# Attention and SwiGLU block, forward and backward, on one core: one burst of loads a group in the backward queue, x and partial sums in the rows of the job operands, row layouts of q and k stored in the forward

## The chip, the core and the metric

The kernel runs on one core of one Trainium2 chip. The core has five engines that run side by side, each with its own queue of instructions: TensorE (PE, matmuls and transposes into PSUM), VectorE (DVE), ScalarE (ACT), GpSimd (POOL) and SyncE (SP). SP does no arithmetic here: it issues most of the DMA transfers, in the order in which they stand in its queue, and POOL issues most of the others. The metric is the time of one execution on the device in microseconds (us), lower is better; the median of several executions counts.

## The reference

The forward is a layer norm followed by two branches that are added to the input, multi-head attention (16 heads of 28, 2048 positions) and a SwiGLU feed-forward (width 448 to 1792). The kernel returns the output and the gradients for x and the five weights.

```python
def _A_ref(x, wqkv, wo):
    ...
    scores = jnp.einsum("bhqd,bhkd->bhqk", q, k) * (Dh ** -0.5)
    p = _softmax(scores, axis=-1)
    o = jnp.einsum("bhqk,bhkd->bhqd", p, v)
    ...
def _B_ref(x, w_gate, w_up, w_down):
    g = _silu(x @ w_gate)
    u = x @ w_up
    return (g * u) @ w_down
x = A_x
xn = _layernorm(x, axis=-1)
return x + _A_ref(xn, A_wqkv, A_wo) + _B_ref(xn, B_w_gate, B_w_up, B_w_down)
...
_out, _vjp = jax.vjp(_f, A_x, A_wqkv, A_wo, B_w_gate, B_w_up, B_w_down)
_grads = _vjp(grad_out)
```

## The kernel before

The kernel has a forward loop, a backward loop and a short final stage. The order of the work is written out by hand; each engine runs its instructions in that order.

**Forward** (from the start to about 690 us). The 16 heads stand in 4 groups `g` of 4 heads, padded to 32 rows each, so that q, k and v of a group are 128 x 2048 tiles (`qT`, `kT`, `vT`, feature by position). The loop runs over `g`, 4 blocks of queries `qc` and 16 blocks of keys `kt`; each step computes scores (L667), their exponential on ACT (L671) and the product with v (L642). Beside it, `fill` takes small pieces of other work from a queue: the projections of the next group, and the feed-forward with its gradients. The feed-forward is cut into 14 slices `fc` of 128 columns and 4 blocks `sc` of positions. At the end of each item (`fc`, `sc`) SP gets one DMA transpose of the tile `hduT` (L474) and three stores of its parts to DRAM tensors, `hO_d`, `da_d` and `du_d` (L477). `hduT` has two buffers.

Twelve weight layouts (`weight_layout`) are made on the way: SP transposes a block of a weight into the tile `w_stage`, which has one buffer (L356, L358), and POOL stores it in DRAM one item later (L357, L359). One is made in each of the slices 1 to 12, at `sc == 1`, first gate, then up, then qkv. `proj_store` stores `qT`, `kT` and `vT` of a group in DRAM.

**Backward** (about 690 to 1510 us). The 512 units run over 8 pairs of heads `pr`, 4 blocks of keys `kc`, and 16 blocks of queries. Eight units make a group `W` (64 of them); `pos` is the place of a unit in its group. For each unit PE computes two score tiles (L962, L972), ACT the exponential `E` (L981), and DVE the product `ds` (L987, one instruction a unit). Two units share a buffer `ds`, and there are 5 such buffers. `ds` is needed in transposed form, `dsT`. Of the four buffers of a group three are transposed by SP (L1014, 512 KB each, at `pos` 2, 4 and 6), the fourth by PE (L901) with two copies on DVE at `pos` 1 of the next group (L903). A buffer `ds` is free again when its transpose has landed and PE has read it.

Each group also carries a **job**, a chain of matmuls that fills PE's gaps: 16 output tiles (`y`), 16 tiles each of two partial sums of the gradient of x (`dx` 0 and 1), and weight gradients (`dwq`). A job needs one block of operands, `ck`, loaded two groups ahead by `job_load` at `pos` 0 (L749 from `hO_d`, L755 from `da_d` or `du_d`). A `y` job adds x, and a `dx` 1 job adds the partial sum of `dx` 0, with one more matmul each; these 112 KB come in a load of their own into `x_c` (L751 from x, L759 from `pA_d`), 32 loads in all. `extra_load` brings, at `pos` 4, one more block in most groups: an operand of the next pair (L613, 256 KB), a row layout of q, k or dO for the next group of heads (`load_rows`, L621 and L623, 512 KB), or a piece of a weight (L603). For q and k, `load_rows` is a DMA transpose from `qT_d` or `kT_d`; for dO it is a plain load, since the forward has stored rows of dO in `spo_d`. `sp_later` holds the transposes of finished sums (L888, L939).

Loads and transposes of the backward all stand in SP's queue. The order in a group is: `ck`, `x_c` at `pos` 0; first transpose of `ds` at `pos` 2; extra load, second transpose at `pos` 4; third transpose at `pos` 6.

At the change from forward to backward the pools of the forward are closed, and the tiles of the backward are placed on the same memory; the first instruction that writes such a tile waits for the last one that used the memory.

Of the kernel before, what the change touches and what calls it, by code (L numbers as in the profile page):

```python
# [13 lines left out]
BF16 = mybir.dt.bfloat16  # L14
# [5 lines left out]
D = 448  # L20
# [3 lines left out]
G = 4  # L24
HP = 32
P = 128
NT = S // P
NFC = F // P
# [10 lines left out]
def kernel(  # L39
# [31 lines left out]
    spo_d = dram.tile([G, P, NT * P], BF16, name="spo_d")  # L71
    hO_d = dram.tile([NT, P, NFC + G, P], BF16, name="hO_d")
    da_d = dram.tile([NT, P, NFC, P], BF16, name="da_d")
    du_d = dram.tile([NT, P, NFC, P], BF16, name="du_d")
    wT_d = dram.tile([2, P, NFC, D], BF16, name="wT_d")
    wqT_d = dram.tile([P, 3 * G, D], BF16, name="wqT_d")
    pA_d = dram.tile([P, NT, D], BF16, name="pA_d")
    pB_d = dram.tile([P, NT, D], BF16, name="pB_d")
# [271 lines left out]
    def weight_layout(i):  # L350
# [8 lines left out]
        return lambda: pool.dma_start(out=wqT_d[:, :, d0:d0 + dn], in_=s_[:, :3 * G, :dn])  # L359

    queue = deque()
    cur = deque()
# [68 lines left out]
    def ffn_items(fc, sc, extra):  # L431
# [35 lines left out]
        def dh(c):  # L467
            mm("dh", lambda c: wdT[fc % 2][:, c, :], dyT, c)
            if c == 3:
                o = st["o"]  # L470
                for wi, src in ((2, "g1"), (1, "w")):
                    dve.scalar_tensor_tensor(out=o[:, :, wi, :], in0=quad(st["dh"]), scalar=0.5, in1=quad(st[src]),
                                             op0=ALU.mult, op1=ALU.mult)
                sp.dma_start_transpose(out=ffn[fc][:, tsl].rearrange("p t w s -> p (t w) s"),  # L474
                                       in_=o[:].rearrange("p t w s -> p (t w s)"))
                for wi, dst in ((0, hO_d), (1, da_d), (2, du_d)):
                    sp.dma_start(out=dst[tsl, :, fc, :].rearrange("k p s -> p k s"), in_=o[:, :, wi, :])  # L477
                if sc == 1 and 1 <= fc <= 12:
                    later.append(weight_layout(fc - 1))
                elif later:  # L480
                    later.pop()()
# [44 lines left out]
    def o_items(g, qc, o_ps):  # L526
# [8 lines left out]
        def tr(i):  # L535
# [3 lines left out]
            if i < 3:  # L539
# [12 lines left out]
                                   in_=O_sp[g][:, tsl, :].rearrange("p t c -> p (t c)"))  # L552
            sp.dma_start(out=hO_d[tsl, :, NFC + g, :].rearrange("k p s -> p k s"),
                         in_=oT[:].rearrange("p (k s) -> p k s", k=4))
# [61 lines left out]
    def load_rows(g, i):  # L616

        t = opn.tile([P, NT, P], BF16, name="Qsp", tag="v_sp") if i == 0 else \
            spg_[0].tile([P, NT, P], BF16, name=("Qsp", "Ksp", "dOsp")[i])
        if i == 2:  # L620
            sp.dma_start(out=t[:].rearrange("p t c -> p (t c)"), in_=spo_d[g])  # L621
        else:
            sp.dma_start_transpose(out=t[:], in_=(qT_d, kT_d)[i][g])  # L623
        spt[g, i] = t
# [23 lines left out]
    for i, (g, qc, kt) in enumerate(steps):  # L648
        if i == NEARLY:
            pro.close()  # L650
            open_ffn()
            proj_store(0)
        if kt == 0 and qc == (1 if g == 0 else 0) and g + 1 < G:
            push(proj_items(g + 1), front=True)
# [33 lines left out]
    while late:  # L688
        push(late.pop(0), front=True)
    fill(1e9)  # L690
    fst.close()
    bst.close()
# [50 lines left out]
    def job_load(i):  # L743
        j = jobs.get(i)
        if j is None:
            return
        if j[0] == "y":
            t = ckp.tile([P, NFC + G, P], BF16, name="ck")
            sp.dma_start(out=t[:], in_=hO_d[j[1]])  # L749
            x = ckp.tile([P, D], BF16, name="x_c")  # L750
            sp.dma_start(out=x[:], in_=x_d[:, j[1], :])  # L751
            chunk[i] = (t, x)
        elif j[0] == "dx":
            t = ckp.tile([P, NFC + G, P], BF16, name="ck")
            sp.dma_start(out=t[:, :NFC], in_=(da_d, du_d)[j[1]][j[2]])  # L755
            x = None
            if j[1] == 1:
                x = ckp.tile([P, D], BF16, name="x_c")
                sp.dma_start(out=x[:], in_=pA_d[:, j[2], :])  # L759
            chunk[i] = (t, x)  # L760

# [57 lines left out]
    def job_mms(i, ps):  # L819
# [5 lines left out]
        if j[0] == "y":  # L825
            t, x = chunk[i]
            out = []
            for n in range(NFC + G):
                rhs = (wtile["wd"][:, n, :] if n < NFC else wo_pad[:, n - NFC, :D])
                out.append(lambda n=n, rhs=rhs: pe.matmul(ps[:, :D], lhsT=t[:, n, :], rhs=rhs,  # L830
                                                          start=(n == 0), stop=False))
            out.append(lambda: pe.matmul(ps[:, :D], lhsT=ident_bf[:], rhs=x[:], start=False, stop=True))
            return out
# [4 lines left out]
        if x is not None:  # L838
            out.append(lambda: pe.matmul(ps[:, :D], lhsT=ident_bf[:], rhs=x[:], start=False, stop=True))
        return out  # L840

    def job_out(i, ps):
# [14 lines left out]
        else:  # L857
            pool.dma_start(out=(pA_d, pB_d)[j[1]][:, j[2], :], in_=o[:])

# [89 lines left out]
    for k in range(N + UW + 4):  # L949
        W, pos = k // UW, k % UW  # L950
        k_now[0] = k
        if k < N:
            pr, kc, w, qi = units[k]
            if pos == 0 and W:
                job_load(W + 2)
            if pos == 4:
                extra_load(W)
# [178 lines left out]
```

## Time and profile before

| | us |
|---|---|
| median of 3 runs | 1562.62 (1561.1 to 1566.55) |
| the profiled execution | 1575.18 |
| its span, first to last instruction | 1573.4 |
| PE busy in the span | 1438.7 (91%) |
| DVE busy | 1121.7 (71%) |
| ACT busy | 1148.8 (73%) |
| POOL busy | 293.6 (19%) |
| transposes of `ds`, issue to landing, median of 192 | 5.9 |

The times that the text takes from the profile belong to the profiled execution, which took 12.6 us longer than the median. The mean granted TensorE clock over the span is 0.958 of full speed. A row of the timeline gives start, duration, engine and line; on SP's queue a duration is the time until the next entry of the queue can be taken, not the time until the data have landed.

### The profile page before, as it was taken

The numbers are of one execution on the slowest core, as the hardware profiler recorded it, in microseconds if no ns is written. First come the engines' busy times: TensorE is split into PE (matmuls) and PEld (weight loads), VectorE is DVE, ScalarE is ACT, GpSimd is POOL, SyncE is SP. The second block draws the span as 40 slices with busy tenths as digits, with TensorE's granted clock in tenths as the row PEclk, the third lists the DMA queues.
The fourth block names the chain that finished last, engine by engine and source line by source line (L and its number), as shares of the span: only waits on it lengthen the run. The fifth ranks groups of instructions, "written<-read, shape, count | busy, mean of one in ns | idle before, by whom it ended". The sixth has DMA issues, their size and how long they took to land.

```text
span 1573.4 us, 31511 instructions
## 1 busy us (share of the span) xinstructions
PE 1438.7 (91%) x12278; PEld 580.1 (37%) x12278; DVE 1121.7 (71%) x1459; ACT 1148.8 (73%) x1312; POOL 293.6 (19%) x479
## 2 busy tenths in 40 slices
PE   6899999999999999979988899889888889999958
PEld 3233333333333333333333335333334333533424
DVE  7465556665666566648777789788888878998925
ACT  4487888887888877757667677668777777777824
POOL 4000111111111110120121122212213122221222
PEclk7688999999999999989999999999999999999979
DMA  5456638765777677859999999999999999999974
GB/s 157 110 123 140 141 76 186 148 148 118 160 147 145 142 156 158 184 138 210 216 219 211 210 195 189 221 212 208 211 214 199 203 213 196 194 213 199 195 205 134
DMA packets 764567, 276.98 MB, mean 176 GB/s; under 512 B 730929, under 2 KB 744049, under 8 KB 764417
## 3 DMA queue, kind: packets, MB, share of 16 engines
q1 hardware_dynamic: 748656, 238.19, 79.1%
q0 software_dynamic: 14960, 36.60, 8.8%
q8 instruction: 96, 1.57, 0.4%
q14 instruction: 55, 0.44, 0.1%
q10 hardware_dynamic: 800, 0.17, 0.1%
HBM read 63.44 MB, written 59.24 MB: 78 GB/s over the span
## 4 chain that ended last, share of the span: by engine, by line
PE 64%; DMA 17%; DVE 8%; ACT 6%; issue 4%; SPq 1%; POOL 0%; DVEq 0%; ACTq 0%; POOLq 0%
DMA dsT<-ds 13%; PE s_ps L667 9%; PE f_ps L412 8%; PE f_ps L438 8%; PE sd L962 6%; PE o_ps L642 5%; ACT E L981 5%; PE acc L875 5%; DVE ds L987 4%; PE aux L916 3%; PE sd L901 3%; PE f_ps L197 3%; PE sd L972 3%; PE sd L1052 2%; PE aux L830 2%
## 5 line engine op out<-in xcount | busy, mean ns | idle before, releaser
L987 DVE TENSOR_TENSOR ds<-sd,E 128x1024 bf16<-128x1024 f32 x512 | 606.4, 1219 | 126.1 <-DMA dsT<-ds 65.9
L981 ACT ACTIVATE E<-sd 128x1024 bf16<-128x1024 f32 x512 | 521.0, 1024 | 199.0 <-PE sd L972 140.8
L671 ACT ACTIVATE eT<-s_ps 128x1024 bf16<-128x1024 f32 x512 | 497.1, 1021 | 143.8 <-PE s_ps L667 142.5
L962 PE MATMUL sd<-KV,QD 32*128 32x512 bf16 x1024 | 202.7, 390 | 45.0 <-DVE ds L987 39.2
L972 PE MATMUL sd<-KV,QD 32*128 32x512 bf16 x1024 | 203.5, 390 | 11.3 <-ACT E L981 5.1
L667 PE MATMUL s_ps<-qT,kT 32*128 32x512 bf16 x1024 | 198.6, 397 | 0.4 <-ACT eT L671 0.4
L875 PE MATMUL acc<-E,dOsp 128*32 128x512 bf16 x1024 | 139.1, 395 | 3.7 <-DMA dOsp<-spo_d 3.7
L875 PE MATMUL acc<-ds,Qsp 128*32 128x512 bf16 x1024 | 139.1, 395 | 0.0
L962 PEld LDWEIGHTS <-QD 32*128 32x128 bf16 x1024 | 58.3, 91 | 206.6 <-issue 193.3
L438 PE MATMUL f_ps<-xnT,wgu 128*128 128x512 bf16 x448 | 122.3, 392 | 8.7 <-DVE w_sb L464 8.7
L836 PE MATMUL aux<-W,ck 128*128 128x448 bf16 x448 | 112.5, 356 | 0.0
L642 PE MATMUL o_ps<-eT,v_sp 128*32 128x512 bf16 x1024 | 104.4, 402 | 4.1 <-DMA v_sp<-vT 4.1
L667 PEld LDWEIGHTS <-kT 32*128 32x128 bf16 x1024 | 47.2, 91 | 164.1 <-issue 160.2
L412 PE MATMUL f_ps<-xn_sp,f_sp 128*128 128x448 bf16 x448 | 98.9, 354 | 0.0
L972 PEld LDWEIGHTS <-QD 32*128 32x128 bf16 x1024 | 69.0, 91 | 60.3 <-issue 56.3
L901 PE MATMUL sd<-ident_bf,ds 128*128 128x128 bf16 x1024 | 70.1, 223 | 20.4 <-DVE ds L987 20.0
L903 DVE COPY dsT<-sd 128x1024 bf16<-128x1024 bf16 x128 | 82.2, 684 | 2.7 <-PE sd L901 2.3
L412 PEld LDWEIGHTS <-f_sp 128*128 128x128 bf16 x672 | 58.9, 98 | 67.0 <-issue 20.2
L916 PE MATMUL aux<-dsT,Ksp 128*32 128x512 bf16 x1024 | 71.2, 398 | 7.3 <-DMA dsT<-ds 7.3
L901 PEld LDWEIGHTS <-ds 128*128 128x128 bf16 x1024 | 62.7, 100 | 35.3 <-issue 35.0
L450 DVE SCALAR_TENSOR_TENSOR g<-t_sb,f_ps 128x512 f32<-128x512 f32 x56 | 38.4, 685 | 46.1 <-ACT t_sb L448 46.1
L932 POOL TENSOR_TENSOR dq_acc<-dq_acc,dq_s 128x512 f32<-128x512 f32 x32 | 40.5, 1265 | 133.9 <-ACT dq_s L928 133.9
(145 smaller groups left out, 1719.8 us busy)
## 6 DMA issues: line engine op xcount, KB each, us to landing
ck<-hO_d SPq DMA_DIRECT2D x16, 576.0 KB, 4.7
hO_d<-hduT SPq DMA_DIRECT2D x56, 128.0 KB, 3.4
da_d<-hduT SPq DMA_DIRECT2D x56, 128.0 KB, 3.0
du_d<-hduT SPq DMA_DIRECT2D x56, 128.0 KB, 3.3
ck<-da_d SPq DMA_DIRECT2D x16, 448.0 KB, 4.5
ck<-du_d SPq DMA_DIRECT2D x16, 448.0 KB, 4.3
dq_c<-dqkv_d SPq DMA_DIRECT2D x8, 768.0 KB, 5.3
dqkv_d<-dkv_o POOLq DMA_DIRECT2D x64, 64.0 KB, 4.2
```

Source lines behind the costliest of these rows:

```text
L412: pe.matmul(acc[:, :D], lhsT=src[:, t, wi, :], rhs=rhs[:, t, :D], start=(t == 0), stop=(t == NT - 1))
L438: pe.matmul(st[name][:], lhsT=w(c), rhs=src[:, tsl, c, :], start=(c == 0), stop=(c == 3))
L642: pe.matmul(o_ps[HP * hh:HP * (hh + 1), :], lhsT=v[:, kt, HP * hh:HP * (hh + 1)], rhs=e[hh // 2][:, hh % 2, :], start=(kt == 0), stop=(kt ...
L667: pe.matmul(s_ps[:, j, :], lhsT=kT[r:r + HP, kt * P:(kt + 1) * P], rhs=qT[r:r + HP, qc * 512:(qc + 1) * 512], start=True, stop=True, tile_ ...
L671: act.activation(out=e[:], in_=s_ps[:], func=ACT.Exp, scale=SCALE)
L875: pe.matmul(acc[r:r + HP, :], lhsT=src[:, qt, 64 * hp + HP * j:64 * hp + HP * j + HP], rhs=m[:, j, :], start=(qt == 0), stop=(qt == NT - 1 ...
L901: pe.transpose(ps[:, u, i, :], ds[:, u, i // 4, (i % 4) * P:(i % 4 + 1) * P], ident_bf[:])
L916: pe.matmul(ps[r:r + HP, :], lhsT=Ks[:, kc * 4 + kt, 64 * hp + HP * j:64 * hp + HP * j + HP], rhs=dsT[:, 4 * s_:4 * s_ + 4, j, kt, :], sta ...
L962: pe.matmul(s_ps[:, j, :], lhsT=q[HP * j:HP * j + HP, qt * P:(qt + 1) * P], rhs=kv[HP * j:HP * j + HP, kc * 512:(kc + 1) * 512], start=Tru ...
L972: pe.matmul(d_ps[:, j, :], lhsT=q[r:r + HP, qt * P:(qt + 1) * P], rhs=kv[r:r + HP, kc * 512:(kc + 1) * 512], start=True, stop=True, tile_p ...
L981: act.activation(out=E[k][:], in_=s_ps[:], func=ACT.Exp, scale=SCALE)
L987: dve.tensor_tensor(out=ds[:, u % 2], in0=d_ps[:], in1=E[u][:], op=ALU.mult)
```

## The change

- The row of `hO_d` gets x behind the operands, and the row of `du_d` the partial sum of `dx` 0. x is copied from DRAM to DRAM once, by POOL, early in the forward. The 32 loads of `x_c` go, and `pA_d` with them; the loads of `ck` get longer rows (5504 and 4480 bytes a partition).
- `extra_load` moves from `pos` 4 to `pos` 0, right behind the load of `ck`.
- The row layouts of q and k are made in the forward: 16 transposes of half a tile into `w_stage` (256 KB each), each stored by POOL in `rows_d`; `load_rows` becomes a plain load for all three. A layout is made at `sc` 1 and at `sc` 3 of every slice, 28 in all: 16 row layouts at set places, and the 12 weight layouts around them, now qkv first, then gate and up. The last eight, gate and up, fall into the slices 10 to 13, and the store of the last one comes after all other work of the forward.

```diff
-    hO_d = dram.tile([NT, P, NFC + G, P], BF16, name="hO_d")
-    da_d = dram.tile([NT, P, NFC, P], BF16, name="da_d")
-    du_d = dram.tile([NT, P, NFC, P], BF16, name="du_d")
+    hO_d = dram.tile([NT, P, (NFC + G) * P + D], BF16, name="hO_d")
+    da_d = dram.tile([NT, P, NFC * P], BF16, name="da_d")
+    du_d = dram.tile([NT, P, NFC * P + D], BF16, name="du_d")
+    rows_d = dram.tile([2, G, P, NT * P], BF16, name="rows_d")
...
+    def row_layout(g, i):
+
+        tq, h = i // 2, i % 2
+        s_ = stg.tile([P, NFC, P], BF16, name="w_stage")
+        sp.dma_start_transpose(out=s_[:, :8, :], in_=qk_tiles[(g, tq)][:, 1024 * h:1024 * (h + 1)])
+        return lambda: pool.dma_start(out=rows_d[tq, g, :, 1024 * h:1024 * (h + 1)],
+                                      in_=s_[:, :8, :].rearrange("p t c -> p (t c)"))
+
+    row_slots = {n: (n - n0, g) for g, n0 in enumerate((0, 4, 9, 16)) for n in range(n0, n0 + 4)}
+    weights = [8, 9, 10, 11] + list(range(8))
+    stages = {}
+    for n in range(2 * NFC):
+        if n in row_slots:
+            stages[(n // 2, 2 * (n % 2) + 1)] = lambda r=row_slots[n]: row_layout(r[1], r[0])
+        else:
+            stages[(n // 2, 2 * (n % 2) + 1)] = lambda w=weights.pop(0): weight_layout(w)
...
-                if sc == 1 and 1 <= fc <= 12:
-                    later.append(weight_layout(fc - 1))
+                if (fc, sc) in stages:
+                    later.append(stages[(fc, sc)]())
                 elif later:
                     later.pop()()
...
-        if i == 2:
-            sp.dma_start(out=t[:].rearrange("p t c -> p (t c)"), in_=spo_d[g])
-        else:
-            sp.dma_start_transpose(out=t[:], in_=(qT_d, kT_d)[i][g])
+        sp.dma_start(out=t[:].rearrange("p t c -> p (t c)"), in_=(rows_d[0], rows_d[1], spo_d)[i][g])
...
             proj_store(0)
+            pool.dma_start(out=hO_d[:, :, (NFC + G) * P:].rearrange("k p d -> p k d"), in_=x_d)
...
     fill(1e9)
+    later.pop()()
     fst.close()
     bst.close()
...
+        w = n * P + (0 if j[:2] == ("dx", 0) else D)
+        t = ckp.tile([P, (NFC + G) * P + D], BF16, name="ck")
+        sp.dma_start(out=t[:, :w], in_=src)
+        chunk[i] = (t[:, :n * P].rearrange("p (n s) -> p n s", s=P), t[:, n * P:w] if w > n * P else None)
...
-            pool.dma_start(out=(pA_d, pB_d)[j[1]][:, j[2], :], in_=o[:])
+            pool.dma_start(out=pB_d[:, j[2], :] if j[1] else du_d[j[2], :, NFC * P:], in_=o[:])
...
             if pos == 0 and W:
                 job_load(W + 2)
-            if pos == 4:
                 extra_load(W)
```

More of the change, by code (lines that the diff above doesn't have):

```diff
@@ L71 @@
     spo_d = dram.tile([G, P, NT * P], BF16, name="spo_d")
-    hO_d = dram.tile([NT, P, NFC + G, P], BF16, name="hO_d")
-    da_d = dram.tile([NT, P, NFC, P], BF16, name="da_d")
-    du_d = dram.tile([NT, P, NFC, P], BF16, name="du_d")
+    hO_d = dram.tile([NT, P, (NFC + G) * P + D], BF16, name="hO_d")
+    da_d = dram.tile([NT, P, NFC * P], BF16, name="da_d")
+    du_d = dram.tile([NT, P, NFC * P + D], BF16, name="du_d")
+    rows_d = dram.tile([2, G, P, NT * P], BF16, name="rows_d")
     wT_d = dram.tile([2, P, NFC, D], BF16, name="wT_d")
     wqT_d = dram.tile([P, 3 * G, D], BF16, name="wqT_d")
-    pA_d = dram.tile([P, NT, D], BF16, name="pA_d")
     pB_d = dram.tile([P, NT, D], BF16, name="pB_d")
@@ L476, in dh @@
                 for wi, dst in ((0, hO_d), (1, da_d), (2, du_d)):
-                    sp.dma_start(out=dst[tsl, :, fc, :].rearrange("k p s -> p k s"), in_=o[:, :, wi, :])
-                if sc == 1 and 1 <= fc <= 12:
-                    later.append(weight_layout(fc - 1))
+                    sp.dma_start(out=dst[tsl, :, fc * P:(fc + 1) * P].rearrange("k p s -> p k s"), in_=o[:, :, wi, :])
+                if (fc, sc) in stages:
+                    later.append(stages[(fc, sc)]())
                 elif later:
@@ L552, in tr @@
                                    in_=O_sp[g][:, tsl, :].rearrange("p t c -> p (t c)"))
-            sp.dma_start(out=hO_d[tsl, :, NFC + g, :].rearrange("k p s -> p k s"),
+            sp.dma_start(out=hO_d[tsl, :, (NFC + g) * P:(NFC + g + 1) * P].rearrange("k p s -> p k s"),
                          in_=oT[:].rearrange("p (k s) -> p k s", k=4))
@@ L747, in job_load @@
         if j[0] == "y":
[L748 to L752, printed above, removed]
-        elif j[0] == "dx":
[L754 to L760, printed above, removed]
+            n = NFC + G
+            src = hO_d[j[1]]
+        elif j[0] == "dx":
+            n = NFC
+            src = (da_d, du_d)[j[1]][j[2]]
+        else:
+            return
+        w = n * P + (0 if j[:2] == ("dx", 0) else D)
+        t = ckp.tile([P, (NFC + G) * P + D], BF16, name="ck")
+        sp.dma_start(out=t[:, :w], in_=src)
+        chunk[i] = (t[:, :n * P].rearrange("p (n s) -> p n s", s=P), t[:, n * P:w] if w > n * P else None)
     def dwq_mms(g, c, ps):
@@ L831, in job_mms @@
                                                           start=(n == 0), stop=False))
-            out.append(lambda: pe.matmul(ps[:, :D], lhsT=ident_bf[:], rhs=x[:], start=False, stop=True))
+            out.append(lambda: pe.matmul(ps[:, :D], lhsT=ident_bf[:], rhs=x, start=False, stop=True))
             return out
@@ L838, in job_mms @@
         if x is not None:
-            out.append(lambda: pe.matmul(ps[:, :D], lhsT=ident_bf[:], rhs=x[:], start=False, stop=True))
+            out.append(lambda: pe.matmul(ps[:, :D], lhsT=ident_bf[:], rhs=x, start=False, stop=True))
         return out
```

## The prediction

> **What bounds the kernel now.** I read the busy windows of the backward first, then the spacing of its groups on DVE, then SP's queue. The columns of the windows are busy us (and instructions) of PE, PEld, DVE, ACT and POOL, the granted clock, the DMA share and GB/s:
>
> ```profile
> 708.00:910.00 202.00, 182.11 (x1715) 71.24 (x1713) 160.04 (x151) 139.89 (x157) 32.42 (x43) 0.97 1.11 214
> 910.00:957.00 47.00, 44.22 (x539) 20.33 (x537) 42.63 (x41) 36.35 (x41) 11.57 (x25) 0.96 1.10 191
> ```
>
> The first stretch holds the groups in which `y` operands are loaded, the second groups without job loads. DVE is busy 79% of the first and 91% of the second. The copies of L903 come once a group, so their starts measure it. The fastest groups take 11.40 us (W = 18, 19, 30). All 63 from W = 1 take 789.9 us, against 63 x 11.40 = 718.2: an excess of 71.7 us. By what is loaded: `y` (W = 1 to 14) 13.52 us each, 29.7 of excess; `dx` 0 (16 groups) 12.47, 17.1; `dx` 1 (16) 12.44, 16.7; no job load (17) 11.89, 8.3. The price of the loads shows; whose it is, the next rows say.
>
> ```profile
> 812.70 1.29 DVE L903 COPY dsT<-sd 128x1024 bf16<-128x1024 bf16 x2
> 820.87 2.36 DVE L987 TENSOR_TENSOR ds<-sd,E 128x1024 bf16<-128x1024 f32 x2 [2.02 <-DMA dsT<-ds]
> 828.13 1.28 DVE L903 COPY dsT<-sd 128x1024 bf16<-128x1024 bf16 x2
> ```
> ```profile
> 822.72 0.53 SPq L749 DMA_DIRECT2D ck<-hO_d  x1
> 823.34 0.39 SPq L751 DMA_DIRECT2D x_c<-in_A_x_dram  x1
> 823.84 4.86 SPq L1014 DMA_TRANSPOSE dsT<-ds  x1
> 828.75 0.58 SPq L613 DMA_DIRECT2D QD<-qT_d  x1
> 829.42 1.22 SPq L939 DMA_TRANSPOSE dq_sp<-dq_o  x1
> 830.74 6.35 SPq L1014 DMA_TRANSPOSE dsT<-ds  x2
> 837.18 0.54 SPq L749 DMA_DIRECT2D ck<-hO_d  x1
> ```
> ```profile
> DVE ds L987 <- DMA dsT<-ds: 65.9, 52, 3.7
> L1014 SPq DMA_TRANSPOSE dsT<-ds x192: 1343/3258/6255, 694.8 to 1501.6; - x192
> L623 SPq DMA_TRANSPOSE Qsp<-qT_d x4: 2311/2370/5733, 607.9 to 1176.2; - x4
> L621 SPq DMA_DIRECT2D dOsp<-spo_d x4: 319/574/642, 700.4 to 1202.5; - x4
> ```
>
> This group takes 15.43 us. SP's rows stand end to end with gaps of 0.1 us: SP is behind. The load at 822.72 belongs to `pos` 0 of W = 9, which DVE passed near 811.5. The transposes run as late, the five buffers of `ds` stay taken, and DVE waits: 65.9 us in 52 waits, nearly the whole excess. So in the loaded groups the bound is the sum of SP's rows, above all the transposes of `ds`, whose row lasts from 1.3 to 6.3 us. What stands ahead decides: over the timeline of the backward the mean is 3.95 us behind an `x_c` load (26 rows), 3.54 behind another plain load (35), and 2.45 behind the transpose of L888 (23). A transpose behind a plain load seems to wait until that load has drained.
>
> **Part by part, the backward.** (a) 32 `x_c` loads go: 0.39 us and a 0.10 gap each. Their bytes stay, in a longer `ck` row, so I count 0.49 and nothing for the data. It pays where SP is behind: all 14 `y` groups, 6.9 us, and about half of the 16 `dx` 1 groups, 3.9. Bounds 0 (bytes alone bind) and 15.7 (all 32). By the Trainium skill, DMA: Bandwidth & Descriptors, section Anatomy of one DMA, a transfer has a fixed cost of about 2.0 us beside its bytes; by that, 32 fewer loads would be 64 us if they ran one by one. Here they overlap: SP is free again after 0.39 us.
>
> (b) The extra load goes to `pos` 0. It leaves the place ahead of the second transpose and joins `ck` ahead of the first, where four units instead of two lie since the last transpose. The second transpose changes from a row behind a load (3.54) to one behind a transpose (2.45 behind a small one; the pair at 830.74 has 3.2 each): 0.3 to 1.1 saved. The first now drains 256 KB more: 0 to 0.7 lost (256 KB at the some 390 GB/s that fine slices of the DMA view show while loads run). I take 0.4 a group: 14 `y` groups 5.6; of the 24 `dx` groups with an extra load half, 4.8. Bounds -5 and +25. Nothing waits behind the moved load that did not before, except the first transpose; its landing at 5.9 us leaves it some 5 us before DVE needs the buffer.
>
> (c) Seven transposes of q and k rows become plain loads (the eighth stands in the forward): rows of 2.37 and 2.77 us become 0.57, 2.0 less; the next transpose then stands behind a load instead of a transpose, 3.54 for the 2.73 of the three such rows, 0.8 back. 1.2 x 7 = 8.4, of which 7 counts. Bounds 0 and 14.
>
> Together 6.9 + 3.9 + 5.6 + 4.8 + 7 = 28 us; range 5 to 50, the top being what DVE's waits leave to gain.
>
> **The hand-over.** Its rows:
>
> ```profile
> 694.71 2.04 POOL L511 DMA_DIRECT2D out_dram<-dwd_sb  x4
> 696.24 3.85 DMA out_dram<-dwd_sb
> 700.36 3.83 DMA dOsp<-spo_d
> 475.22 1.09 POOL L357 DMA_DIRECT2D wT_d<-w_stage  x1 [0.69 <-issue]
> ```
>
> In the built program the first `ds` of the changed kernel lies on the memory of `w_stage` and waits for the last layout's store, which POOL issues behind the four of L511: at 696.8. Such a narrow store landed after 4.1 and 4.5 us, so at 701; before, the first `ds` began at 692.1. The eight units of W = 0 take 10 us, as before. The first transpose waits for two units, 703.6; its row of 3.2 us stands ahead of the `dOsp` load, which lands 4.4 later, at 711.2. PE, which waited for it until 704.5 before, goes on 6.7 us later. Everything behind on SP (two `ck`, the k rows) moves along; nobody needs it sooner. Cost 6.7, bounds 4 and 9.4 (the whole delay of `ds`).
>
> **The forward.** 16 row layouts come in. Half-tile transposes have no row; between 1.2 (the 128 KB ones) and 2.4 us (512 KB), I take 1.8: 29 us of SP, 16 POOL stores. PE hides them: it is busy 243.3 of 250 us from 400 to 650, and SP's rows fill some 35 us of every 50. Without that cover they would cost all 29. The copy of x (1.8 MB, POOL, behind the stores of q, k and v) competes near 75 us with loads for the first slices: 0, at most 3. In the last slices the cover is thin: DVE waited 8.7 us for `du_d` stores of `hduT` after 560. There the q rows fall from 5.73 us to 0.6, though `hduT` was ready only 1.9 us before that row ended: 1.9 gained. A gate or up layout is added after (12, 3), 1.7 to 2.2, ahead of stores that DVE needs: 1.9 lost. Those at (13, 1) and (13, 3) delay nothing that PE needs before 665. Half of the rows of `hO_d` and `du_d` now start 128 bytes off a multiple of 256. By the Trainium skill, same page, section How a descriptor splits into AXI transactions, such a 256-byte piece is cut in two; by that, as an estimate, the 2.7 us landings in the last slices would grow by some tenths; no run here shows it yet. I count 1 us for the forward, bounds -4 and +12.
>
> **Sum.** -28 + 6.7 + 1 = -20 us: span 1573.4 to 1553, execution 1575.2 to 1555. Taken from the median, 1562.6 - 20 = 1543.
>
> **Rivals.** *The bytes bind.* SP is only held up by full DMA engines: then (a) and (b) move nothing, (c) saves 5, and with the hand-over's 6.7 and 1 the time is 1565; with half of (a) and (b), 1555. For it: the DMA digits read 9 through the backward. Against: drops to near 0 GB/s lie within those slices and groups without job loads move only 191 GB/s yet run at 11.4. Middle 1560.
>
> *The forward pays, slower.* One buffer `w_stage`, two layouts a slice: in slices 10 to 13 SP stands at L356 until POOL's store has landed (up to 6.7 us after issue), and `hduT` with its two buffers stops DVE and PE. Four more layouts of 2.2 us through that chain: 9; three more stalls of 2 us further ahead: 6; hand-over 9; backward only -12: +12, 1575. It decides when a layout's SP row lies over 5 us behind the one it should follow. For it: the chain already runs through four `du_d` stores between 617 and 642. Against: stores are issued a whole item ahead.
>
> *All of the waiting goes.* The burst takes every late transpose away: -55 + 8 = 1516. For it: groups with only transposes and one load run at 11.4. Against: groups with `dx` loads and nothing else after W = 52 still show 14.73 once.
>
> **Chances.** Forecast 0.52, the bytes 0.18, the forward 0.22, all 0.08. A measurement here tells 0.3% (4.7 us) from no change. Faster: 0.52 + 0.08 + a third of the bytes = 0.65; same 0.12; slower 0.23. The forecast's own range is 1528 to 1557; with part of the rivals, 1524 to 1573.
>
> **What would show it.** Group spacing at L903 in the `y` groups down from 13.5 to 12.5; DVE's wait on `dsT` from 65.9 to about 35; the second transpose's row near 2.6; first `ds` about 10 us (before 1.6) after PE's first backward matmul; `du_d` waits after 560 about as before. Wrong if `y` groups stay above 13, if rows behind `ck` plus extra load grow by over 1 us, or if PE in the forward loses more than 5 us.

## The result, and the profile after

The changed kernel takes 1577.3 us in the median (1571.88 to 1579.75), the kernel before, measured beside it, 1561.82 (1559.97 to 1566.55). The ratio is 1.0092, with a 95% interval of 1.0066 to 1.0117: slower by about 14 us. The prediction, 1543, had the wrong sign.

The profiled execution took 1577.18 us, its span is 1575.4. That is only 2 us more than the profile shown of before, because that profile came from an execution 12.6 us above its median. A second profile of before (span 1557.5) is therefore used below as well.

| us | before | before, second | after |
|---|---|---|---|
| DVE's last forward copy (`dwd_sb`) ends | 690.5 | 679.5 | 700.6 |
| from there to the first copy of `dsT` (L903, now L917) | 18.2 | 18.8 | 23.6 |
| the 63 groups | 789.9 | 786.5 | 782.2 |
| one group with a `y` load, mean | 13.52 | 13.56 | 13.38 |
| last copy of `dsT` to the last row on DVE, SP or POOL | 72.4 | 70.3 | 66.6 |

The busy windows of the same two stretches of the backward, with the same columns as before:

```profile
723.50:925.50 202.00, 180.82 (x1741) 71.08 (x1737) 161.44 (x154) 140.65 (x158) 32.42 (x43) 0.98 1.11 216
925.50:972.50 47.00, 44.41 (x527) 20.52 (x527) 42.07 (x41) 36.11 (x42) 11.60 (x25) 0.93 1.11 191
```

DVE is busy 80% of the first and 90% of the second, against 79% and 91%: the loaded groups are nearly as slow as they were. SP's queue in such a group, to be held against the rows from 822.72 on:

```profile
837.07 0.53 SPq L773 DMA_DIRECT2D ck<-hO_d  x1
837.65 0.46 SPq L630 DMA_DIRECT2D QD<-qT_d  x1
838.21 6.37 SPq L1027 DMA_TRANSPOSE dsT<-ds  x1
844.68 1.21 SPq L953 DMA_TRANSPOSE dq_sp<-dq_o  x1
845.98 5.88 SPq L1027 DMA_TRANSPOSE dsT<-ds  x2
```

One load row is gone, and the two transposes behind `dq_sp` take 2.94 each instead of 3.18. But the first transpose, now behind both loads, takes 6.37 instead of 4.86. The view of DVE's waits (total, times, longest) says the same; its last row here is that of before:

```profile
DVE ds L1000 <- DMA dsT<-ds: 66.3, 52, 3.6
DVE hduT L479 <- DMA du_d<-hduT: 25.9, 13, 5.4
...
DVE hduT L462 <- DMA du_d<-hduT: 16.7, 9, 4.7
```

The wait for `dsT` was 65.9 (58.8 in the second profile) and is 66.3. The wait for the `du_d` stores of the forward, 16.7 and 9.4 in the two profiles of before, is 25.9. A new stall of PE stands at the start of the forward. SP's rows there before, then SP, POOL and PE after, from the timeline; the bracket is the idle time before and what ended it:

```profile
67.06 6.75 SPq L310 DMA_TRANSPOSE dyT<-dy_sp  x1
73.99 6.08 SPq L316 DMA_TRANSPOSE woT<-wo_pad  x4
```

```profile
66.06 11.42 SPq L310 DMA_TRANSPOSE dyT<-dy_sp  x1
77.67 12.52 SPq L316 DMA_TRANSPOSE woT<-wo_pad  x4
...
66.77 1.20 POOL L667 DMA_DIRECT2D hO_d<-in_A_x_dram  x1
...
90.97 1.03 PE L577 MATMUL f_ps<-woT,dyT 128*128 128x128 bf16 x8 [8.55 <-DMA woT<-wo_pad]
```

The copy of x is issued at 66.77 and lands 23.5 us later. While it runs, the five transposes take 23.9 us; before they took 12.8. PE stands for 8.55 us. In the stretch 80 to 100 PE (the first column after the length) is busy 11.45 us at a granted clock of 0.63; in the second profile of before, the row below, it is busy all 20 at 1.00, in the first all 20 at 0.83.

```profile
80.00:100.00 20.00, 11.45 (x60) 4.09 (x58) 6.59 (x16) 6.27 (x7) 0.57 (x1) 0.63 0.96 153
```
```profile
80.00:100.00 20.00, 20.00 (x138) 7.34 (x137) 11.89 (x22) 16.07 (x17) 1.64 (x4) 1.00 0.38 86
```

At the hand-over, the chain of waits:

```profile
706.88 3.46 DMA wT_d<-w_stage
711.79 2.36 DVE ds L1000 x2
715.08 4.48 DMA dOsp<-spo_d
720.04 2.32 PE acc L889 x15
```

The first `ds` waits for the store of the last layout, and the `dOsp` load and PE follow, as predicted.

### The profile page after: what moved, and what is told of

It is laid out like the page before. It is cut to its first block, busy times and chain, and to the rows that moved or that the text cites. A ratio compares the mean times of both kernels' runs of the same rounds, so it can differ in the third digit from the quotient of the medians.

```text
span 1575.4 us, 31504 instructions
## 1 busy us (share of the span) xinstructions
PE 1436.0 (91%) x12278; PEld 581.4 (37%) x12278; DVE 1120.8 (71%) x1459; ACT 1148.6 (73%) x1312; POOL 303.2 (19%) x496
## 4 chain that ended last, share of the span: by engine, by line
PE 61%; DMA 22%; DVE 7%; ACT 5%; issue 3%; SPq 2%; POOL 0%; DVEq 0%; ACTq 0%; POOLq 0%
DMA dsT<-ds 18%; PE s_ps L682 9%; PE f_ps L429 8%; PE f_ps L455 8%; PE o_ps L656 5%; PE sd L975 5%; ACT E L994 4%; PE acc L889 4%; PE f_ps L197 3%; DVE ds L1000 3%; PE sd L985 3%; PE aux L930 2%; PE sd L1065 2%; PE sd L915 2%; PE aux L844 2%
## 5 line engine op out<-in xcount | busy, mean ns | idle before, releaser
L1000 DVE TENSOR_TENSOR ds<-sd,E 128x1024 bf16<-128x1024 f32 x512 | 605.9, 1219 | 125.3 <-DMA dsT<-ds 66.3
L985 PE MATMUL sd<-KV,QD 32*128 32x512 bf16 x1024 | 203.7, 390 | 12.4 <-ACT E L994 6.2
L889 PE MATMUL acc<-E,dOsp 128*32 128x512 bf16 x1024 | 135.3, 386 | 1.3 <-DMA dOsp<-spo_d 1.3
L889 PE MATMUL acc<-ds,Qsp 128*32 128x512 bf16 x1024 | 135.3, 386 | 0.0
L917 DVE COPY dsT<-sd 128x1024 bf16<-128x1024 bf16 x128 | 82.1, 683 | 2.3 <-PE sd L915 2.0
```

The lines of the kernel that those rows point to most:

```text
L889: pe.matmul(acc[r:r + HP, :], lhsT=src[:, qt, 64 * hp + HP * j:64 * hp + HP * j + HP], rhs=m[:, j, :], start=(qt == 0), stop=(qt == NT - 1 ...
L985: pe.matmul(d_ps[:, j, :], lhsT=q[r:r + HP, qt * P:(qt + 1) * P], rhs=kv[r:r + HP, kc * 512:(kc + 1) * 512], start=True, stop=True, tile_p ...
L1000: dve.tensor_tensor(out=ds[:, u % 2], in0=d_ps[:], in1=E[u][:], op=ALU.mult)
```

## The experiments

Each kernel ran in five rounds beside the kernel before, on the same chip, but not all on one chip; so all numbers are ratios to the kernel before, with 95% intervals. 0.001 is 1.6 us. Differences of two ratios carry the root of the sum of the squares of their half-widths.

**A second profile of before** (no edit).

> The kernel before once more, for a second profile. The first profiled execution took 1575, 12.6 us over the median of 1562. Theory (the excess lay in the backward and the final stage, in late transposes of ds): the forward's last matmuls end near 684 again, the 63 groups take 775 to 785 us instead of 789.9 and the final stage 69 instead of 74.8. Rival (the excess was somewhere in the forward): PE's last forward matmul ends near 675 and the groups take 790 again. If the theory holds, the changed kernel's 782.2 us for the 63 groups is no saving at all.

It is the second column of the table above. Of the 15.9 us between the two spans 11.0 lay before the end of the forward, 3.4 in the groups and 2.1 in the last stage; the hand-over was 0.6 longer. So the first theory was mostly wrong and its rival mostly right: the last copy ends at 679.5, and the groups take 786.5. Against that, the changed kernel's groups save 4 to 8 us, not 28.

**The copy of x later**

```diff
+        if i == 60:
+            pool.dma_start(out=hO_d[:, :, (NFC + G) * P:].rearrange("k p d -> p k d"), in_=x_d)
         if i == NEARLY:
...
-            pool.dma_start(out=hO_d[:, :, (NFC + G) * P:].rearrange("k p d -> p k d"), in_=x_d)
```

> The changed kernel, with the copy of x issued at step 60 of the forward (near 205 us, DMA share 0.48) instead of step 12 (near 67 us). Theory (the copy holds up the transposes of dyT and wo for the first slices, and PE with them): the early loss of about 8 us goes, 1577 becomes 1569, du_d in the chain at 116 instead of 124. Rival (the late start of PE is hidden by what PE waits for later, or comes from the row layouts): 1575 to 1578.

1.0013 (0.9997 to 1.003): 0.0079 +- 0.0030 less than the changed kernel, 12.3 us. SP's rows are back:

```profile
63.61 6.71 SPq L310 DMA_TRANSPOSE dyT<-dy_sp  x1
70.51 5.44 SPq L316 DMA_TRANSPOSE woT<-wo_pad  x4
```

PE is busy 20.00 of the 20 us from 80 to 100, at clock 1.00. The gain is above the 8 expected. The clock may be the rest. In the changed kernel PE is busy all the time from 91.0 to 105.4 us at a granted clock of 0.50; at full clock that work would take half as long, an estimate of 7 us beside the 8.55. The Trainium skill, TensorE: Matmul & The Clock Gate, section What's actually happening, says that the gate passes half the pulses after one idle window of about 3.4 us; the clock of 0.50 around a stall of 8.55 agrees. How much of it the copy costs is not shown: the first profile of before has 0.50 too, from 69.7 to 86.5, without such a stall.

**The store of the last layout earlier** (with the late copy)

```diff
-    ffn_list += pend
+    ffn_list += pend[:1] + [[(0.0, lambda: later.pop()())]] + pend[1:]
...
     fill(1e9)
-    later.pop()()
```

> As the run with the late copy, and the store of the last weight layout stands in the queue of forward work behind the first of the last weight gradients instead of behind all of them. Theory (the first ds waits for this store): the first ds comes some 5 us sooner after PE's last forward matmul, PE's accumulation starts 5 us sooner, 1569 becomes 1564. Rival (the delay is used up by something else at the hand-over, as the first loads): within 1.5 us of the run with the late copy.

0.9989 (0.9963 to 1.0015), 0.0024 +- 0.0031 less: too little for the times alone. The profile is clear. From DVE's last forward copy to the first `ds` it is 10.0 us with the late copy alone and 1.7 here, as before. To the first copy of `dsT` it is 24.1 and 18.3: 5.7 us. In the later kernels with this store and `ck` on SP it is 18.2 to 19.5.

**The burst undone** (with both repairs)

```diff
                 job_load(W + 2)
+            if pos == 4:
                 extra_load(W)
```

> As the run with both repairs, with the extra load back at place 4 of the group, ahead of the second transpose. Theory (the drain of the extra load is paid by whichever transpose stands behind it, so the burst moves it and saves nothing): within 3 us of the run with both repairs, the first transpose's row shorter and the second's longer by the same. Rival as predicted (the burst saves 10 us): 10 slower. Second rival (two loads in one burst make the first transpose later than it makes the second sooner): 4 to 8 faster.

0.9953 (0.9931 to 0.9974), and when run again later 0.9976 (0.9951 to 1.0); their mean, 0.9964 +- 0.0016, is "the reference" below. Against 0.9989 that is 0.0025 +- 0.0031. The 63 groups take 776.4 and 776.8 us instead of 782.3, `y` groups 13.05 and 13.01 instead of 13.44, and SP's queue shows how:

```profile
822.42 0.66 SPq L773 DMA_DIRECT2D ck<-hO_d  x1
823.18 4.36 SPq L1028 DMA_TRANSPOSE dsT<-ds  x1
827.59 0.58 SPq L630 DMA_DIRECT2D QD<-qT_d  x1
828.26 1.84 SPq L953 DMA_TRANSPOSE dq_sp<-dq_o  x1
830.19 5.21 SPq L1028 DMA_TRANSPOSE dsT<-ds  x2
```

With the extra load away, the first transpose takes 4.36 instead of 6.37, and the others do not pay it back. Counted row by row over the 14 `y` groups, the first transpose of a group takes 4.49 us on average here and 5.34 with the burst, the second 3.58 and 3.15, the third about 2.7 in both. That is no chance of one profile: eleven profiles with merged loads and no burst have 4.35 to 4.70 and 3.47 to 3.66, the three with the burst 5.31 to 5.51 and 3.04 to 3.15. So the burst does shorten the second, by 0.4 us, but lengthens the first by 0.9. How much the groups gain by undoing it is less certain: with the late copy alone, where the burst stands, all 63 take 777.8 us.

**The burst alone, in the kernel before**

```diff
                 job_load(W + 2)
-            if pos == 4:
                 extra_load(W)
```

> The kernel before with one edit: the extra load at place 0 instead of 4, behind ck and x_c. Step (b) of the prediction alone: 10 us saved, 1552, ratio 0.993. Theory after the runs so far (putting both loads ahead of the first transpose costs 5): 1565 to 1570, ratio 1.002 to 1.006, y groups no faster. Second rival (no effect): 0.999 to 1.001.

0.9981 (0.9955 to 1.0008): no effect that can be told. The groups take 788.7 (786.5 and 789.9 without), `y` groups 13.25 instead of 13.5, `dx` 0 groups 12.70 instead of 12.46; the wait for `dsT` is 62.2. Step (b) and the theory after the first runs both fall; the second rival is nearest. In the `y` groups the first transpose takes 4.29 us (4.01 and 4.14 without), the second 2.84 (3.42 and 3.53): here the second gains more than the first loses. The burst moves the delay between transposes; it gains nothing that can be told in the kernel before, and the small loss in the changed one is not proved. Why the first transpose loses more in the changed kernel, with the same bytes ahead of it, stays open.

**The 32 loads separate again** (reference with one more load a job, same rows in DRAM)

```diff
-        sp.dma_start(out=t[:, :w], in_=src)
+        sp.dma_start(out=t[:, :n * P], in_=src[:, :n * P])
+        if w > n * P:
+            sp.dma_start(out=t[:, n * P:w], in_=src[:, n * P:w])
```

> The run with both repairs and without the burst (1555), with the 112 KB of x or of the partial sum loaded by a load of their own again, from the same longer DRAM rows, right behind ck: 32 loads more, the same bytes. Step (a) of the prediction priced these at 10.8 us. Theory (SP pays for each load): 1561 to 1566, y groups from 13.05 to 13.5. Rival (bytes alone bind, the number of loads is free): 1554 to 1557.

1.0002 (0.9978 to 1.0025), 0.0037 +- 0.0028 above the reference: 5.9 us, 0.18 us a load. The number of loads is not free, but cheaper than the 0.34 on average (10.8 us for 32) of step (a). With two loads the first transpose of a `y` group takes 4.19 us, with the one longer load 4.49 (4.43 in the second run): some 0.3 of the 0.49 us that a load row and its gap took come back there.

**Merged operands alone** (the kernel before with this part of the change and the late copy of x, nothing else)

```diff
-            x = ckp.tile([P, D], BF16, name="x_c")
-            sp.dma_start(out=x[:], in_=x_d[:, j[1], :])
...
-                sp.dma_start(out=x[:], in_=pA_d[:, j[2], :])
...
+        sp.dma_start(out=t[:, :w], in_=src)
```

> The kernel before with x and the partial sums in the rows of the operands (copy of x late) and nothing else: no row layouts in the forward, q and k rows by transposes, extra load at place 4. Step (a) of the prediction alone. If the 32 loads are worth the 7 us that the run with split loads gave: ratio 0.994 to 0.997. If the run with split loads misled: 0.999 to 1.001. Against the run that differs from it by the row layouts in the forward alone (1.0042) it prices these: theory 4 to 8 us (0.003 to 0.005 lower), the prediction's step 1 us.

0.9963 (0.9939 to 0.9986): 5.8 us, the same as from the other side. The first transpose of a `y` group takes 4.40 us, 4.01 and 4.14 in the kernel before.

**The rows of q and k transposed in the backward again** (reference, whose forward still makes the row layouts)

```diff
-        sp.dma_start(out=t[:].rearrange("p t c -> p (t c)"), in_=(rows_d[0], rows_d[1], spo_d)[i][g])
+        if i == 2:
+            sp.dma_start(out=t[:].rearrange("p t c -> p (t c)"), in_=spo_d[g])
+        else:
+            sp.dma_start_transpose(out=t[:], in_=(qT_d, kT_d)[i][g])
```

> The run with both repairs and without the burst (1555), with the row layouts of q and k made by DMA transposes in the backward again; the forward still makes and stores its own, which nothing reads. Step (c) priced this at 7 us, and the hand-over is as it was. Theory (step (c) right): 1560 to 1563, rows of the layouts 2.4 to 2.8 instead of 0.5. Rival (the seven groups have slack): 1554 to 1557.

1.0042 (1.0014 to 1.007), 0.0078 +- 0.0032 above the reference: step (c) is worth 12 us, more than the 7 predicted. The groups take 784.9 instead of 776.6. This kernel differs from the one with merged operands alone only by what the forward does for the row layouts, and costs 0.0079 +- 0.0037 more: 12 us for the forward, where the prediction had 1. What (c) gains, its preparation takes back: the reference and the kernel with merged operands alone are at 0.9964 and 0.9963. Both 12s rest on this one kernel's 1.0042; the profiles say less for each, 8 us in the groups and, for the forward, 6.5 (the last copy ends at 689.4 us on average in ten profiles with 28 layouts and the late copy, at 682.9 in four with 12).

**Fewer bytes in the `y` loads** (reference, 9 of 18 operand blocks loaded and each used twice, so that the output `y` is another one)

```diff
+        z = n * P // 2 if j[0] == "y" else 0
...
-        sp.dma_start(out=t[:, :w], in_=src)
+        sp.dma_start(out=t[:, z:w], in_=src[:, z:w])
...
-                out.append(lambda n=n, rhs=rhs: pe.matmul(ps[:, :D], lhsT=t[:, n, :], rhs=rhs,
+                out.append(lambda n=n, rhs=rhs: pe.matmul(ps[:, :D], lhsT=t[:, 9 + n % 9, :], rhs=rhs,
```

> The run with both repairs and without the burst, where a y job loads only 9 of its 18 operand blocks, and multiplies each twice: 288 KB of 688 KB are left out of each of 16 loads, PE's work and SP's number of rows stay. It prices bytes. Theory (the DMA engines are full in the y stage): y groups from 13.05 to 11.9 to 12.3, time 10 to 16 us less than with full loads, the row of the first transpose from 4.1 to about 3. Rival (the number of transfers on SP counts, bytes do not): y groups 12.8 to 13.1, time within 3 us.

0.9859 (0.9828 to 0.9891), 0.0105 +- 0.0035 below the reference: 16 us for 16 x 288 KB. `y` groups take 11.98 us, nearly as little as groups without a job load. DVE's waits:

```profile
DVE ds L1002 <- DMA dsT<-ds: 27.0, 26, 2.6
```

As many rows on SP, 42% of the `y` bytes left out, and the wait for `dsT` goes from 52.9 (48.3 when run again) to 27.0. The first transpose of a `y` group goes from 4.49 to 3.39 us; the second, behind the extra load, stays at 3.5. The bytes bind in the `y` groups.

**`ck` loaded by POOL** (reference)

```diff
-        sp.dma_start(out=t[:, :w], in_=src)
+        pool.dma_start(out=t[:, :w], in_=src)
```

> The run with both repairs and without the burst (1555), with the loads of ck issued by POOL instead of SP; order and bytes stay. Theory A (a transpose waits for the plain load that stands ahead of it in its own queue): the first transpose's row falls from 4.1 to 2.5 to 3, y groups to about 12, time 1535 to 1545. Theory B (what holds the transpose up are the DMA engines, which the load fills from any queue): rows stay within 0.5 of 4.1 or the later transposes take it over, 1553 to 1560. Theory C (POOL issues too late behind its sums and stores): DVE or PE wait for ck, 1560 to 1580.

1.0062 (1.0031 to 1.0093), slower. The `y` groups take 13.02 us, as with SP. The load no longer stands ahead of the transpose in its queue, and yet:

```profile
825.89 1.22 SPq L953 DMA_TRANSPOSE dq_sp<-dq_o  x1
827.21 9.92 SPq L1028 DMA_TRANSPOSE dsT<-ds  x3
```

Three transposes at 3.31 each. In the `y` groups the first takes 2.62 us instead of 4.49, as theory A said, but the second 4.78 instead of 3.58 and the third 3.46 instead of 2.75: the sum is 10.9 instead of 10.8. All 192 rows together take 653 us instead of 624. So theory A falls, and it is B's second half that holds: the data of the load delay the transposes from any queue. The Trainium skill, DMA: Bandwidth & Descriptors, section Queues, rings and completion order, says that each engine takes a queue's descriptors in order and turns between queues packet by packet. That fits: POOL's queue changes which transposes the load delays, not how long the engines are taken. In the profile the hand-over takes 23.1 us instead of 19.5 and the groups 781.3 instead of 776.4; being from the fastest execution (1565.8), it does not show the rest of the way to the median's 1576, and that stays open.

**DRAM rows padded to multiples of 256 bytes** (reference)

```diff
-    hO_d = dram.tile([NT, P, (NFC + G) * P + D], BF16, name="hO_d")
+    hO_d = dram.tile([NT, P, (NFC + G) * P + D + 64], BF16, name="hO_d")
...
-    du_d = dram.tile([NT, P, NFC * P + D], BF16, name="du_d")
+    du_d = dram.tile([NT, P, NFC * P + D + 64], BF16, name="du_d")
```

> The run with both repairs and without the burst (1555), with the DRAM rows of hO and du lengthened by 128 bytes, so that all of them start at a multiple of 256 bytes. Theory (alignment does not matter here): 1553 to 1557, landings of the hO and du stores the same within 0.1 us. Rival (pieces that start 128 bytes off are cut in two and the stores of the last slices are slow by it): the DVE wait for du_d stores falls from 28.8 to the 10 to 17 of the kernel before, 1549 to 1552.

0.9975 (0.9947 to 1.0003), no difference from the reference. The stores of `hduT` land after 3.3, 3.1 and 3.3 us, with 3.3, 3.2 and 3.3 unpadded, and the wait for `du_d` is 23.7, not 10 to 17. So the cut pieces that the prediction took from the Trainium skill cost nothing that shows here.

**All layouts early** (late copy, no burst; the last layout falls in slice 9)

```diff
+    rows = [(g, i) for g in range(G) for i in range(4)]
+    first = (0, 6, 14, 24)
...
+    for n in range(3 * NFC):
+        if rows and n >= first[rows[0][0]]:
+            stages[(n // 3, n % 3 + 1)] = lambda r=rows.pop(0): row_layout(*r)
+        elif weights:
+            stages[(n // 3, n % 3 + 1)] = lambda w=weights.pop(0): weight_layout(w)
...
+                if later:
+                    later.pop()()
                 if (fc, sc) in stages:
                     later.append(stages[(fc, sc)]())
-                elif later:
-                    later.pop()()
```

> The changed kernel with the late copy of x and without the burst; the 28 layouts are made in three of the four items of a slice, as early as q and k of a group are there, so that the last falls into slice 9 and no store is left for the end of the forward. Compare with the run with both repairs and without the burst (ratio to before 0.9953), where DVE waits 28.8 us for du_d stores and PE is busy 238 of 250 us from 400 to 650. Theory (the eight gate and up layouts of slices 10 to 13 hold up the stores that free hduT): the wait falls to 10 to 17, PE regains 3 to 6, ratio 0.991 to 0.994. Rival (the total of SP's or the DMA engines' work in the forward counts, not its place): wait stays above 25, ratio 0.994 to 0.997.

1.0029 (1.0005 to 1.0054), 0.0065 +- 0.0029 above the reference, the opposite of the theory. The wait for `du_d` is 68.6 us, and PE is busy 331.9 of the 350 us from 150 to 500 instead of 347.8. SP, POOL and DVE:

```profile
419.69 0.56 SPq L495 DMA_DIRECT2D du_d<-hduT  x1
424.22 1.49 SPq L356 DMA_TRANSPOSE w_stage<-in_B_w_up_dram  x1
...
419.62 1.09 POOL L357 DMA_DIRECT2D wT_d<-w_stage  x1 [0.68 <-issue]
...
439.01 0.69 DVE L480 SCALAR_TENSOR_TENSOR hduT<-g,f_ps 128x512 bf16<-128x512 f32 x1 [8.01 <-DMA du_d<-hduT]
```

The store of a layout is now issued in the item in which the next layout is made, just ahead of it. SP stands from 420.25 to 424.22: the one buffer `w_stage` is free only when POOL's store has landed. The next weights and the transposes of `hduT` queue behind, and DVE waits 8.01 us. This is the mechanism of the prediction's slower rival: 71.6 us of gaps ahead of the 28 layouts. In the changed kernel these gaps sum to 2.5 us. Its layouts never stand, so that rival's mechanism did not act there.

**Where the forward loses: three edits of the reference.** Row layouts of the last heads put last, so that the heavier weight layouts move to slices 6 to 11:

```diff
-    row_slots = {n: (n - n0, g) for g, n0 in enumerate((0, 4, 9, 16)) for n in range(n0, n0 + 4)}
+    row_slots = {n: (n - n0, g) for g, n0 in enumerate((0, 4, 9, 24)) for n in range(n0, n0 + 4)}
```

> As the reference run, with the order of the layouts changed: the four row layouts of the last group (256 KB each) come last, in slices 12 and 13, and the gate and up layouts (448 KB) that stood there move forward to slices 6 to 11. Theory (heavy layouts in the last slices, where the DMA engines are full, make the stores of hduT late): the du_d wait falls from about 28 to below 20, forward 2 to 4 us shorter, ratio 0.992 to 0.994. Rival (the number of layouts counts): within 0.0015 of the reference.

0.9964 (0.9939 to 0.999), and the reference beside it:

> The run with both repairs and without the burst once more, as the reference of the three beside it. Ratio 0.9953 again within 0.003. PE's last forward matmuls near 690 and DVE's wait for du_d stores 25 to 30, if these belong to the kernel and not to one execution.

0.9976, as said; the wait for `du_d` was 26.1, the last copy ended at 685.2. The order of the layouts makes no difference that can be told (0.0012 +- 0.0035; wait 25.2).

No layouts of the last heads (24 in slices 0 to 11, two transposes back in the backward):

```diff
-    row_slots = {n: (n - n0, g) for g, n0 in enumerate((0, 4, 9, 16)) for n in range(n0, n0 + 4)}
+    row_slots = {n: (n - n0, g) for g, n0 in enumerate((0, 4, 9)) for n in range(n0, n0 + 4)}
...
-    for n in range(2 * NFC):
+    for n in range(24):
...
+        if i < 2 and g == G - 1:
+            sp.dma_start_transpose(out=t[:], in_=(qT_d, kT_d)[i][g])
```

> As the reference run, with no row layouts for the last group of heads: its q and k rows are transposed in the backward as in the kernel before, and the forward makes 24 layouts, all in slices 0 to 11, none in 12 and 13. Theory (the forward's loss of 7 to 10 us falls in slices 12 and 13): du_d wait 8 to 15 as in the kernel before, forward 5 us shorter than the reference, backward 3 longer, ratio 0.992 to 0.994. Rival (each layout costs wherever it stands): forward 2 shorter, backward 3 longer, ratio 0.995 to 0.998.

0.9948 (0.9931 to 0.9965), 0.0028 +- 0.0030 below the reference beside it. From 600 to 650 PE is busy 48.38 us (43.06 and 42.40 in the two runs of the reference), though the wait for `du_d` is still 22.6 in all, not the 8 to 15 of the theory. Forward: last copy at 681.7. Backward: groups 782.0, 5 longer. Suggestive, not proved.

A third buffer of `hduT`, paid for with two of `eT`:

```diff
-    ep = bst.enter_context(tc.tile_pool(name="ep", bufs=7))
+    ep = bst.enter_context(tc.tile_pool(name="ep", bufs=5))
...
-        for nm, n in (("fT", 2), ("spp", 2), ("ftmp", 2), ("fout", 2), ("op_", 2), ("op1", 1)):
+        for nm, n in (("fT", 3), ("spp", 2), ("ftmp", 2), ("fout", 2), ("op_", 2), ("op1", 1)):
```

> As the reference run, with three buffers of hduT instead of two, paid for with five buffers of eT instead of seven. Theory (the forward loses because a store of hduT that is one layout late stops DVE at its two buffers): the du_d wait falls below 8, PE is busy above 245 of 250 us from 400 to 650, ratio 0.988 to 0.992. Rival (the DMA engines are full there, a third buffer only moves the wait to f_sp, or fewer eT buffers cost as much): ratio 0.994 to 1.000.

0.9928 (0.9902 to 0.9954), 0.0048 +- 0.0036 below the reference. The wait is gone:

```profile
DVE hduT L479 <- DMA du_d<-hduT: 2.4, 1, 2.4
```

So a store that comes late stops DVE through the two buffers. That the stores come late because more is ahead of them fits the rows, but is argued: 28 layout rows of 46 to 48 us in all on SP instead of 12 of 23, and rows of the `hduT` transposes after 500 us of 2.4 us on average (2.3 in the reference's first run) instead of 1.7. The same windows, with merged operands alone and then with row layouts (the reference's first run):

```profile
600.00:650.00 50.00, 47.00 (x285) 17.22 (x282) 33.85 (x58) 36.56 (x41) 5.28 (x8) 0.97 0.87 169
```
```profile
600.00:650.00 50.00, 43.06 (x245) 15.12 (x243) 29.64 (x50) 32.19 (x37) 6.39 (x9) 0.91 1.01 196
```

The DMA share goes from 0.87 to 1.01 (the last two columns are DMA share and GB/s), PE loses 4 of 47 us, and the granted clock falls from 0.97 to 0.91. With the third buffer the share is still 1.02 and PE is busy 45.92.

**The fastest versions.** Third buffer and 24 layouts together; and, for the balance of the row layouts, merged operands alone with the third buffer:

> Both helps together: no row layouts for the last group of heads (as the run with 24 layouts) and three buffers of hduT (five of eT). Theory (both take the same loss of the forward, the wait for du_d stores and full DMA engines in the last slices): not additive, ratio 0.990 to 0.993. Rival (they take different losses): 0.987 to 0.990.

> The run with merged operands alone (no row layouts in the forward, 0.9963), with three buffers of hduT and five of eT. It tells whether the row layouts pay once their forward cost is covered. Theory (their backward gain of 8 us or more is real, the forward's third buffer is worth 2 or 3 us here): ratio 0.993 to 0.996, above the run beside it by 0.003. Rival (the third buffer was worth as much without row layouts, and these gain nothing): equal to the run beside it within 0.0015.

0.9888 (0.9857 to 0.9918, median 1547.9) and 0.9912 (0.9881 to 0.9943, median 1552.2). The first lies in its rival's range, that the two helps add up, but its interval reaches into the theory's. It beats the kernel before by 17 us and, by the ratios, the changed one by some 32. The second keeps no row layouts at all, and the two are not told apart (0.0024 +- 0.0043): whether the row layouts pay once the forward is covered stays open. Without row layouts the third buffer gains 0.0051 +- 0.0039 (0.9963 to 0.9912), as much as with all of them (0.0048 +- 0.0036). So it helps, but it does not take back what the row layouts cost in particular, and through which wait their 12 us are lost is not shown. That five buffers of `eT` cost nothing was not tried by itself.

## Why the prediction was wrong

| step | predicted, us | measured, us | from |
|---|---|---|---|
| copy of x | 0, at most 3 | +12.3 +- 4.7 | late copy |
| rest of the forward | +1 | +12.4 +- 5.7 | rows transposed again, against merged operands alone |
| (a) 32 loads gone | -10.8 | -5.9 +- 4.4 | split loads; alone -5.8 +- 3.7 |
| (b) burst | -10.4 | +3.8 +- 4.8 | burst undone; alone -3.0 +- 4.1 |
| (c) plain loads of rows | -7 | -12.1 +- 5.0 | rows transposed again |
| hand-over | +6.7 | +3.7 +- 4.8; profile +4.8 to +5.7 | store earlier |
| sum | -20 | +14 | 1577.3 against 1561.8 |

The rows are the differences of one chain of kernels from before to after, apart from (a), and so they add up to the result by construction. The two rows of the forward make the wrong sign: +25 us where the prediction had +1. In the backward three parts gain some 14 us instead of 28. All three of the prediction's signs of being wrong came: `y` groups above 13, the row behind both loads over 1 us longer, and a loss of PE in the forward above 5 us.

**The bound.** It was right that SP's late transposes hold up DVE, and that a transpose's row depends on what stands ahead. The step that failed is the conclusion drawn from it: "A transpose behind a plain load seems to wait until that load has drained", so that the bound is the sum of SP's rows and what one row saves is gained. Then a load moved or merged would free the transpose behind it, `y` groups would go to 12.5 and DVE's wait to 35; they stayed at 13.38 and 66.3. With `ck` on another queue the first transpose is indeed faster, but the next two lose as much, and with fewer bytes in the same number of rows the `y` groups fall to 11.98. So in the `y` groups it is the data that the engines have to move that makes SP's rows long: the rival "the bytes bind". In the `dx` groups no bytes were left out. The rival's evidence could not have told it apart. The DMA share is 1.07 to 1.11 in every stretch of the backward looked at, with `y` loads, without, and with 42% left out. Only leaving bytes out told. (A small slip: the fastest groups take 11.37 us, W = 37 and 51, and the last 10.73, not 11.40; the excess and its shares hardly change.)

**(a)** was right in sign, and the size about half. The term that failed is "nothing for the data": the first transpose behind the longer load takes some 0.3 us more, of the 0.49 counted.

**(b)** failed in "I take 0.4 a group". It counted on 0.3 to 1.1 from the second transpose, and that came (0.4 in the `y` groups, 3.58 to 3.15); but it counted on 0 to 0.7 lost at the first, and that lost 0.9 (4.49 to 5.34). In the `y` groups of the kernel before the first lost only 0.2, and there the burst gained 0.3 us a `y` group, but lost 0.2 a `dx` 0 group. The second row, expected "near 2.6", is 3.09 in the `y` groups of the changed kernel.

**(c)** was right in sign and rather too small. Its cost, though, stood in the forward.

**The hand-over** was right: predicted 6.7 through the store, the first `ds`, the first transpose and `dOsp`, measured 4.8 to 5.7 in the profiles. The first `ds` came 10.0 us after PE's first backward matmul, as said.

**The forward** failed twice. The copy of x, which "competes near 75 us with loads for the first slices: 0, at most 3", was held against loads and not against the five transposes that PE's next matmul needs: they took 23.9 us instead of 12.8. And "PE hides them" held from 150 to 500 (347.8 us busy, both before and after) but not after: from 500 to 650 PE is busy 138.2 to 142.4 us in ten runs with the late copy, all 28 layouts at two a slice and two buffers of `hduT`; 144.6 to 145.8 in four without row layouts; 144.2 in the changed kernel, whose forward runs later there. The prediction had seen that the cover is thin there, and took the gain of a q row, 1.9, against one layout, 1.9, instead of pricing all 16 more layouts. That they cost is measured; whether by their bytes, their rows on SP or their stores is not separated.

The slower rival, 1575, came closest in time, but by luck, not by its mechanism: its stalls at L356, 15 us, did not occur, and the copy, which it did not count, cost 12.3.

## What to carry to other kernels

Where a queue's rows get long, find out whether the queue or the DMA engines are full before moving loads about: leave out bytes, or issue the load elsewhere, and see whether the sum of the rows changes, not only the row behind the load. A copy with no deadline still has a place; put it where the DMA share is low and no transpose is awaited. Work that is taken out of a loaded stage costs what it costs in the stage that takes it; price it there. One more buffer of the tile that late stores hold up (here `hduT`) was worth some 8 us with this work and without it.

## What was not expected of the hardware

A DRAM-to-DRAM copy of 1.8 MB from POOL's queue nearly doubled the time of transposes in SP's queue (12.8 to 23.9 us) for its 23.5 us, with no queue in common; issued at 180 to 195 us, the same copy landed after 10 to 11. 288 KB left out of a load saved 1.0 us of its group, but one load fewer with the same bytes only 0.18. In the prediction the Trainium skill's fixed cost of about 2.0 us a transfer was set aside as overlapped, and the 0.18 agrees; that section describes DMAs that GpSimd issues, and these loads are SP's. And two profiled executions of the same kernel differed by 16 us, 11 of them in the forward, which is as much as the whole effect of this change: a difference of two single profiles proves nothing of this size.
